# Shifting weight preparation between GpSimd, TensorE, ScalarE and VectorE in an attention plus two-MLP kernel, with a new written-out order

## The chip, the core and the metric

One Trainium2 core runs the whole program. Its engines are TensorE (PE in the profile, with its weight loads as PEld), VectorE (DVE), ScalarE (ACT), GpSimd (POOL) and SyncE (SP, which issues the DMAs). The metric is device time in microseconds (us). Three timed runs of the kernel before gave 652.4, 654.35 and 654.43 us, median 654.35. The profiled execution took 653.11 us, of which 651.3 us lie between its first and its last instruction.

## The reference

```
attention: q, k, v  (2 batches, 8 heads, 576 tokens, 64 wide)
  scores = q @ k^T / 8;  kth = 32nd largest of each row
  scores below kth -> -1e9;  attn = softmax;  x = attn @ v     -> 1152 tokens x 512
layer 1:  h = x @ w_in (512 x 2048);   g = max(0.01 h, h);          x = g @ w_out (2048 x 512)
layer 2:  h = x @ w_in2;               g = h * tanh(softplus(h));   out = g @ w_out2
```

## The kernel before

The 1152 tokens are nine tiles of 128, each with eight heads, so there are 72 slots (tile, head). For a slot PE makes 576 scores (line 676), ACT copies them to SBUF in two halves (678), and DVE finds the 32 largest: four `MAX8` (691), each of which yields eight, with three `MATCH_REPLACE8` (694) between them that strike out what was found. GpSimd makes two small scalars from the largest and the 32nd (709, 711), ACT masks and exponentiates (714, 715), PE multiplies with v. After a tile's eighth head DVE normalises its x (778), and the two layers follow, each in four groups: `ph` products (822 to 824) and `y` products (831 to 833). Every float32 operand there is split into a float16 high half and a float16 low half, and three products are summed.

The weights arrive as 16 groups q of 512 x 512 words (0 to 3 and 4 to 7 for layer 1, 8 to 11 and 12 to 15 for layer 2). Each word is 64 bits wide in memory, and the value is put together from its high and its low 32 bits. `load_w` does that in pieces of 1024 words per partition, as the tuple `CV` says for each group: with 1, DVE makes two passes over the high word (389, 395), ACT brings the top bits of the low word into place (382), and GpSimd adds them in, 256 elements at a time (`add`, 331). With 2, DVE makes its second pass as a bare mask (392), and GpSimd adds that too. With 0, DVE does it all in three passes (389, 395, 400), and neither ACT nor GpSimd takes part.

`split_w` takes a group's sum of squares on PE (`gram`, 411), reduces it over the partitions by a product with `ones` (415), makes a power-of-two scale from it and splits the group, as the tuple `LO` says. With 3, ACT writes the high half (433), GpSimd makes a diagonal matrix of the scale (431), PE forms the negated low half as diagonal times raw plus identity times high (436 in float32, 437), and ACT evicts it (438). With 0, ACT scales the raw words in place (459) and copies the high half out (460), and GpSimd subtracts the two (462, or 454 for four groups that are done in place).

The order on each engine is not left to a scheduler: `ORDER` lists for every engine the numbers of its instructions in the sequence in which they are to stand, and `put_in_order` ties each to the one ahead of it. So an engine whose next instruction waits does nothing else, even if later ones could run. Score buffers (`sc`) number three, so the scores of a slot can be copied out only when the slot three earlier has been masked.

Of the kernel before, what the change touches and what calls it, by code (L numbers as in the profile page):

```python
# [9 lines left out]
BF16 = mybir.dt.bfloat16  # L10
# [9 lines left out]
        """22 25 20+2 23 19 26+4 24 35+2 42+2 30 38 37 31 44 32 45+11 33 57+2 56 40 39 34 60 62 59 61 69 63+2 68 67 73  # L20
# [4 lines left out]
        186 185 187 183 189+2 188 191+3 195+2 194 197+4""",  # L25
    "Activation":
        """1 6 2 7 4 3 5 9 8 20 16 10+2 45+2 17 12 18+2 21 13+2 27+2 22 15 29 47 23 39 30 24+2 40 33 41 48+2 31 35 34
# [29 lines left out]
        865 868+4 874+2 879+2 876+3 881+5 889 886+3 890+6""",  # L57
    "Pool":
# [133 lines left out]
def topk_attention_moe_moe2_kernel(  # L192
# [17 lines left out]
    nc = tc.nc  # L210
    P = 128
# [43 lines left out]
    one = cpool.tile([P, 1], F32, name="one")  # L255
# [827 lines left out]
    n = NS  # L1083
# [36 lines left out]
```

## Time and profile before

| what | us |
|---|---|
| timed runs, median of 3 | 654.35 |
| profiled execution, whole | 653.11 |
| profiled execution, first to last instruction | 651.3 |
| busy: PE, DVE, ACT, POOL | 594.3, 541.7, 540.2, 400.7 |

An engine's busy time is the sum of the stretches in which it worked. PE's instructions overlap (each matmul of 128 columns is shown for 220 ns, while the next starts 56 ns later), so its share is read together with the distance between starts. The rows that follow are cut by stretch because different engines are full at different times. The clock (PEclk) is the granted TensorE clock: 1.00 is 2.4 GHz, 0.5 is 1.2 GHz.

### The profile page before, as it was taken

The page shows a single profiled execution, that of the slowest core. Times are in us where ns is not written, and L with a number is a line of the kernel's source. Part 1 is how long each engine was busy: PE and PEld are TensorE (multiplying, and loading weights), DVE is VectorE, ACT ScalarE, POOL GpSimd, SP SyncE. Part 2 cuts the span into 40 slices and gives each one's busy share as a digit, 9 for nine tenths or more (in the row PEclk, how much of TensorE's full clock was granted, in tenths as well). Part 3 has the DMA queues.
Part 4 walks back from the last instruction along what each step waited for, and adds up shares of the span by engine and source line. Part 5 has one row for each costly group of instructions (what it writes and reads, how often), then busy time and mean ns, then how long its engine had stood idle before and what let it go on. Part 6 is the DMA issues. An engine that isn't in the chain of part 4 may idle for free.

```text
span 651.3 us, 16588 instructions
## 1 busy us (share of the span) xinstructions
PE 594.3 (91%) x6420; PEld 434.6 (67%) x6420; DVE 541.7 (83%) x1172; ACT 540.2 (83%) x1011; POOL 400.7 (62%) x594
## 2 busy tenths in 40 slices
PE   2468778989798999999999999999999999999997
PEld 1234545567677887777687777767776877777673
DVE  3998999999999999999999999999999989320232
ACT  4679898999989999999987998897997898752663
POOL 2989986797967745755654566575656575631430
PEclk9999798989899999999999999999999999999999
DMA  8483466553354201444446224253455424210000
GB/s 272 149 314 129 148 209 207 169 166 130 130 165 147 97 23 33 80 82 109 90 77 117 48 60 81 54 84 74 91 71 92 85 48 77 56 33 18 17 2 33
DMA packets 109359, 66.22 MB, mean 102 GB/s; under 512 B 93792, under 2 KB 99936, under 8 KB 109280
## 3 DMA queue, kind: packets, MB, share of 16 engines
q1 hardware_dynamic: 109280, 65.16, 39.0%
q8 instruction: 50, 0.82, 0.5%
q14 instruction: 29, 0.24, 0.1%
HBM read 41.16 MB, written 2.36 MB: 67 GB/s over the span
## 4 chain that ended last, share of the span: by engine, by line
PE 51%; DVE 21%; ACT 18%; issue 4%; DMA 3%; POOL 1%; SPq 1%; POOLq 0%; DVEq 0%; ACTq 0%
DVE top L691 7%; PE ph L822 7%; PE ph L824 7%; PE ph L823 7%; DVE wk L694 7%; PE y L831 6%; PE y L833 6%; PE y L832 6%; PE sps L676 3%; ACT wk L715 2%; DVE warena L395 2%; PE lp L436 2%; DMA rawkr<-in_k_dram 1%; ACT sc L678 1%; DVE warena L389 1%
## 5 line engine op out<-in xcount | busy, mean ns | idle before, releaser
L822 PE MATMUL ph<-xt,warena 128*128 128x128 f16 x1152 | 202.9, 220 | 1.9 <-ACT lk L845 1.1
L823 PE MATMUL ph<-xt,warena 128*128 128x128 f16 x1152 | 203.9, 220 | 0.0
L824 PE MATMUL ph<-xt,warena 128*128 128x128 f16 x1152 | 203.1, 221 | 0.0
L691 DVE MAX8 top<-wk 128x8 f32<-128x576 f32 x216 | 160.7, 753 | 2.7
L331 POOL TENSOR_TENSOR warena<-warena 128x256 int32<-128x256 int32 x136 | 109.5, 832 | 19.3 <-ACT warena L382 6.6
L823 PEld LDWEIGHTS <-warena 128*128 128x128 f16 x1152 | 113.3, 98 | 8.9 <-issue 3.1
L822 PEld LDWEIGHTS <-warena 128*128 128x128 f16 x1152 | 113.5, 99 | 7.6 <-issue 1.4
L824 PEld LDWEIGHTS <-warena 128*128 128x128 f16 x1152 | 113.2, 99 | 2.0 <-issue 0.4
L831 PE MATMUL y<-warena,gg 128*128 128x512 f16 x288 | 109.3, 380 | 0.9 <-DVE gg L863 0.9
L832 PE MATMUL y<-warena,gg 128*128 128x512 f16 x288 | 109.2, 379 | 0.0
L833 PE MATMUL y<-warena,gg 128*128 128x512 f16 x288 | 109.2, 379 | 0.0
L694 DVE MATCH_REPLACE8 wk<-top,wk 128x576 f32<-128x576 f32 x144 | 106.7, 742 | 0.0
L676 PE MATMUL sps<-kst,qst 128*128 128x288 f16 (+1 forms) x320 | 64.3, 299 | 11.7 <-ACT sc L678 10.3
L714 ACT ACTIVATE wk<-sc,nb,iv 128x576 f32<-128x576 f32 x72 | 62.5, 868 | 13.4 <-POOL nb L709 13.3
L678 ACT COPY sc<-sps 128x288 f32<-128x288 f32 x144 | 55.3, 398 | 12.0 <-PE sps L676 11.3
L860 DVE SCALAR_TENSOR_TENSOR mc<-mc,gg 128x512 f32<-128x512 f32 x36 | 26.5, 736 | 45.0 <-ACT mc L859 44.8
L846 POOL TENSOR_TENSOR gg<-lk,gg 128x512 f16<-128x512 f32 x36 | 41.7, 1159 | 34.1 <-ACT lk L845 34.0
L715 ACT ACTIVATE wk<-wk,nb 128x576 f32<-128x576 f32 x72 | 56.1, 779 | 4.3 <-POOL nb L711 2.9
L691 DVE MAX8 top<-sc 128x8 f32<-128x576 f32 x72 | 53.9, 749 | 3.4 <-ACT sc L678 2.1
L694 DVE MATCH_REPLACE8 wk<-top,sc 128x576 f32<-128x576 f32 x72 | 53.4, 742 | 0.0
L709 POOL TENSOR_SCALAR nb<-top,iv 128x2 f32<-128x2 f32 x72 | 25.6, 356 | 39.0 <-DVE top L691 31.3
L831 PEld LDWEIGHTS <-gg 128*128 128x128 f16 x288 | 28.3, 98 | 31.0 <-issue 2.1
(186 smaller groups left out, 1430.3 us busy)
## 6 DMA issues: line engine op xcount, KB each, us to landing
warena<-in_moe_w_in_dram SPq DMA_DIRECT2D x16, 1024.0 KB, 5.4
warena<-in_moe_w_out_dram SPq DMA_DIRECT2D x13, 1024.0 KB, 4.9
warena<-in_moe_w_out_dram SPq DMA_DIRECT2D x6, 512.0 KB, 3.7
out_dram<-o SPq DMA_DIRECT2D x9, 256.0 KB, 2.3
rawkv<-in_v_dram SPq DMA_DIRECT2D x8, 256.0 KB, 3.4
qr<-in_q_dram SPq DMA_DIRECT2D x8, 256.0 KB, 3.6
warena<-held SPq DMA_DIRECT2D x8, 256.0 KB, 2.9
rawkr<-in_k_dram SPq DMA_DIRECT2D x6, 256.0 KB, 3.6
```

The lines of the kernel that those rows point to most:

```text
L331: nc.gpsimd.tensor_tensor(out=o[:, a:a + PIECE], in0=o[:, a:a + PIECE], in1=x[:, a:a + PIECE], op=ALU.add)
L676: nc.tensor.matmul(sps[p0:p0 + n, :HS], lhsT=lq[:, c, p0:p0 + n], rhs=rk[:, half * HS:(half + 1) * HS], start=(c == 0), stop=(c == 1))
L691: nc.vector.max(out=top[:, 8 * r:8 * r + 8], in_=src)
L694: nc.vector.match_replace(out=wk, in_to_replace=top[:, 8 * r:8 * r + 8], in_values=src, imm_value=NEG)
L714: nc.scalar.activation(e, sc, AF.Prelu, bias=nb[:, 1:2], scale=iv, alpha=1e30)
L715: nc.scalar.activation(e, e, AF.Exp, bias=nb[:, 2:3], accum_out=self.sums[:, h:h + 1])
L822: nc.tensor.matmul(o, lhsT=wb, rhs=xa, start=(c == 0), stop=False)
L823: nc.tensor.matmul(o, lhsT=wa, rhs=xb, start=False, stop=False)
L824: nc.tensor.matmul(o, lhsT=wa, rhs=xa, start=False, stop=(c == KC - 1))
L831: nc.tensor.matmul(y, lhsT=gb, rhs=whi(j), start=(g == 0 and f == 0), stop=False)
L832: nc.tensor.matmul(y, lhsT=ga, rhs=wlo(j), start=False, stop=False)
L833: nc.tensor.matmul(y, lhsT=ga, rhs=whi(j), start=False, stop=(g == FG - 1 and f == 3))
```

## The change

Three things change in the code, and the written-out order with them. The new file is 13 lines shorter above these places, so its line numbers are 13 lower: what was 389, 392, 395, 400, 462, 691 and 694 is 376, 379, 382, 387, 449, 678 and 681 in the new order's rows.

- `CV`: groups 1, 5, 6, 8, 10 and 12 go from 1 to 0, and group 3 from 2 to 0.
- `LO`: groups 1, 3, 5, 6 and 8 go from 3 to 0.
- The products with `ones`, which sum a per-partition number over the partitions for k, v, x and each weight group, take the upper 16 bits of both operands as bfloat16, in place of float32.

```diff
-    ones = one.to_broadcast([P, P])
+    ones = one.bitcast(BF16)[:, 1:2].to_broadcast([P, P])
...
     def total(part, n, where=ps_p, tag="p"):
...
-        nc.tensor.matmul(t[:, :n], lhsT=ones, rhs=part, start=True, stop=True)
+        nc.tensor.matmul(t[:, :n], lhsT=ones, rhs=part.bitcast(BF16)[:, 1::2], start=True, stop=True)
...
-    CV = (2, 1, 1, 2, 2, 1, 1, 1, 1, 1, 1, 1, 1, 1, 0, 1)
+    CV = (2, 0, 1, 0, 2, 0, 0, 1, 0, 1, 0, 1, 0, 1, 0, 1)
...
-    LO = (3, 3, 3, 3, 3, 3, 3, 3, 3, 3, 0, 0, 0, 0, 0, 0)
+    LO = (3, 0, 3, 0, 3, 0, 0, 3, 0, 3, 0, 0, 0, 0, 0, 0)
...
-        nc.tensor.matmul(gram[:, P:P + 1], lhsT=ones, rhs=part, start=True, stop=True)
+        nc.tensor.matmul(gram[:, P:P + 1], lhsT=ones, rhs=part.bitcast(BF16)[:, 1::2], start=True, stop=True)
...
 ORDER = {
     "SP":
-        """22 25 20+2 23 19 26+4 24 35+2 42+2 30 38 37 31 44 32 45+11 33 57+2 56 40 39 34 60 62 59 61 69 63+2 68 67 73
+        """21 20 22 19 25 28+2 27 26 23+2 35+2 42 38 43 37 31 44 30 45+2 48 47 34 49 51 50 52 55 54 53 32 39 56 33 58
...
```

Counted over the whole order, GpSimd loses 64 adds of 256 and five diagonals and gains 20 subtractions of 512; ACT loses 14 moves of low words (382), 20 evictions (438) and ten high halves (433) and gains ten scalings (459) and ten copies (460); PE loses 20 float32 diagonal products (436) and 20 identity products (437); DVE gains 14 third passes (400) and two second passes (395) and loses two masks (392).

On DVE, at the start of the program, from the second half of the first keys to the first `MAX8` on scores; before:

```order
L615 SCALAR_TENSOR_TENSOR qn<-qr,qs,qn 128x4x64
L389 TENSOR_SCALAR warena<-warena 128x1024
L392 TENSOR_SCALAR warena<-warena 128x1024
L389 TENSOR_SCALAR warena<-warena 128x1024
L395 SCALAR_TENSOR_TENSOR warena<-warena 128x1024
L389 TENSOR_SCALAR warena<-warena 128x1024
L264 TENSOR_SCALAR u<-tot 128x1
L267 TENSOR_SCALAR ks<-u 128x1
L395 SCALAR_TENSOR_TENSOR warena<-warena 128x1024
L271 TENSOR_SCALAR k_i<-u 128x1
L540 SCALAR_TENSOR_TENSOR kn<-rawkv,ks,kn 128x5x64
L691 MAX top<-sc 128x8 x2
```

and now:

```order
L602 SCALAR_TENSOR_TENSOR qn<-qr,qs,qn 128x4x64
L258 TENSOR_SCALAR k_i<-u 128x1
L376 TENSOR_SCALAR warena<-warena 128x1024
L379 TENSOR_SCALAR warena<-warena 128x1024
L602 SCALAR_TENSOR_TENSOR qn<-qr,qs,qn 128x4x64
L678 MAX top<-sc 128x8
L376 TENSOR_SCALAR warena<-warena 128x1024
L681 MATCH_REPLACE wk<-top,sc 128x576
L379 TENSOR_SCALAR warena<-warena 128x1024
L678 MAX top<-wk 128x8
L681 MATCH_REPLACE wk<-top,wk 128x576
L678 MAX top<-sc 128x8
```

Five passes over weights (389, 395 and the mask 392) stood between the second query half and the first search for maxima; now the search begins directly behind that half and the passes stand between its steps.

On DVE, further on among the weight groups, where searches and passes alternate; before:

```order
L694 MATCH_REPLACE wk<-top,wk 128x576
L389 TENSOR_SCALAR warena<-warena 128x1024
L264 TENSOR_SCALAR u<-gram 128x1
L395 SCALAR_TENSOR_TENSOR warena<-warena 128x1024
L691 MAX top<-wk 128x8
L264 TENSOR_SCALAR u<-qpart 128x1
L267 TENSOR_SCALAR qs<-u 128x1
L267 TENSOR_SCALAR w_s<-u 128x1
L694 MATCH_REPLACE wk<-top,wk 128x576
```

and now:

```order
L382 SCALAR_TENSOR_TENSOR warena<-warena 128x1024
L678 MAX top<-wk 128x8 x2
L681 MATCH_REPLACE wk<-top,wk 128x576 x2
L678 MAX top<-wk 128x8
L387 SCALAR_TENSOR_TENSOR warena<-warena 128x1024
L251 TENSOR_SCALAR u<-qpart 128x1
L376 TENSOR_SCALAR warena<-warena 128x1024
L681 MATCH_REPLACE wk<-top,sc 128x576
L254 TENSOR_SCALAR qs<-u 128x1
L678 MAX top<-wk 128x8 x2
L602 SCALAR_TENSOR_TENSOR qn<-qr,qs,qn 128x4x64
L382 SCALAR_TENSOR_TENSOR warena<-warena 128x1024
```

A piece of weights now takes three passes (376, 382 and 387) in place of two, and two searches stand interleaved more often than one behind itself.

On POOL, at the scalars of the first slots (709 and 711, now 696 and 698), with the adds (331, now 318) around them; before:

```order
L331 TENSOR_TENSOR warena<-warena 128x256 x2
L662 TENSOR_SCALAR iv<-k_i,qi 128x1
L331 TENSOR_TENSOR warena<-warena 128x256 x8
L431 TENSOR_SCALAR diag<-identf,w_s 128x128
L331 TENSOR_TENSOR warena<-warena 128x256 x2
L711 TENSOR_SCALAR nb<-nb 128x1
L331 TENSOR_TENSOR warena<-warena 128x256 x2
L709 TENSOR_SCALAR nb<-top,iv 128x2
L331 TENSOR_TENSOR warena<-warena 128x256
L711 TENSOR_SCALAR nb<-nb 128x1
```

and now:

```order
L696 TENSOR_SCALAR nb<-top,iv 128x2 x2
L698 TENSOR_SCALAR nb<-nb 128x1 x2
L449 TENSOR_TENSOR warena<-warena 128x512
L418 TENSOR_SCALAR diag<-identf,w_s 128x128
L449 TENSOR_TENSOR warena<-warena 128x512
L649 TENSOR_SCALAR iv<-k_i,qi 128x1
L449 TENSOR_TENSOR warena<-warena 128x512 x2
L318 TENSOR_TENSOR warena<-warena 128x256 x12
L696 TENSOR_SCALAR nb<-top,iv 128x2
L698 TENSOR_SCALAR nb<-nb 128x1
```

The two scalars of a slot now stand one behind the other, where adds and a diagonal stood between them, and subtractions of 512 (449) stand among the adds.

On PE the counts of layer products ahead of each slot's scores hardly move: ahead of slot 23's scores stood 312 `ph` and 50 `y` products, now 312 and 55; ahead of the last slot's 2652 and 624, now 2629 and 624, of 3456 and 864 in all. On SP the first keys are now the first two transfers; they were the third and fourth.

## Rows read from the trace of the kernel before

**Rows 1.** The page: busy time by engine, and the chain by engine

```profile
PE 594.3 (91%) x6420; PEld 434.6 (67%) x6420; DVE 541.7 (83%) x1172; ACT 540.2 (83%) x1011; POOL 400.7 (62%) x594
...
PE 51%; DVE 21%; ACT 18%; issue 4%; DMA 3%; POOL 1%; SPq 1%; POOLq 0%; DVEq 0%; ACTq 0%
```

**Rows 2.** Busy time by stretch: length; PE, PEld, DVE, ACT, POOL; clock; DMA

```profile
0.00:25.00 25.00, 7.44 (x43) 4.98 (x44) 13.47 (x26) 14.91 (x25) 10.56 (x17) 1.00 0.75 257
25.00:75.00 50.00, 35.58 (x198) 21.67 (x198) 46.40 (x91) 38.48 (x68) 46.14 (x65) 0.97 0.52 179
75.00:150.00 75.00, 64.59 (x413) 42.48 (x412) 71.56 (x151) 68.87 (x117) 60.61 (x87) 0.93 0.56 185
150.00:225.00 75.00, 67.64 (x659) 53.46 (x658) 73.89 (x158) 71.51 (x132) 58.95 (x73) 0.98 0.41 137
225.00:556.00 331.00, 328.40 (x4098) 247.83 (x4097) 315.35 (x709) 294.42 (x585) 193.56 (x316) 1.00 0.39 73
556.00:651.30 95.30, 90.62 (x1017) 64.14 (x1014) 21.08 (x42) 52.06 (x89) 30.88 (x39) 1.00 0.11 26
```

**Rows 3.** The chain of work from 150 to 160: start, length, what

```profile
154.23 0.77 ACT wk L715 x2
155.00 1.04 ACT warena L459
```

**Rows 4.** Lines, shapes apart: count, busy us, mean ns, idle before

```profile
L331 POOL TENSOR_TENSOR warena<-warena 128x256 int32<-128x256 int32 x136 | 109.5, 832 | 19.3 <-ACT warena L382 6.6 <-DVE warena L392 4.6 <-DVE w_s L267 2.6
...
L436 PE MATMUL lp<-warena,diag 128*128 128x512 f32 x80 | 44.5, 656 | 3.3 <-POOL diag L431 2.0 <-ACT warena L438 1.3
...
L382 ACT ACTIVATE warena<-warena 128x1024 int32<-128x1024 uint16 x28 | 32.0, 1159 | 0.0
L395 DVE SCALAR_TENSOR_TENSOR warena<-warena 128x1024 int32<-128x1024 int32 x23 | 31.0, 1348 | 0.3
...
L389 DVE TENSOR_SCALAR warena<-warena 128x1024 int32<-128x1024 int32 x29 | 27.0, 932 | 3.9 <-PE lp L436 1.7 <-DMA warena<-in_moe_w_in_dram 1.6 <-PE lp L437 0.3
...
L438 ACT ACTIVATE warena<-lp 128x512 f16<-128x512 f32 x40 | 23.4, 596 | 1.6 <-PE lp L437 1.6
L433 ACT ACTIVATE warena<-warena,w_s 128x1024 f16<-128x1024 f32 x20 | 23.0, 1152 | 0.6 <-DVE w_s L267 0.5
...
L392 DVE TENSOR_SCALAR warena<-warena 128x1024 int32<-128x1024 int32 x6 | 6.5, 1086 | 0.1
...
L462 POOL TENSOR_TENSOR warena<-warena 128x512 f16<-128x512 f32 x4 | 5.6, 1416 | 0.0
...
L459 ACT ACTIVATE warena<-warena,w_s 128x1024 f32<-128x1024 f32 x2 | 2.3, 1153 | 0.0
...
L460 ACT CAST warena<-warena 128x1024 f16<-128x1024 f32 x2 | 2.1, 1075 | 0.0
```

**Rows 5.** DVE in order of time, 81 to 92: start, length, what

```profile
81.45 0.74 DVE L694 MATCH_REPLACE8 wk<-top,sc 128x576 f32<-128x576 f32 x1
82.23 0.76 DVE L691 MAX8 top<-wk 128x8 f32<-128x576 f32 x1
...
85.17 1.65 DVE L395 SCALAR_TENSOR_TENSOR warena<-warena 128x1024 int32<-128x1024 int32 x1
86.73 0.75 DVE L691 MAX8 top<-wk 128x8 f32<-128x576 f32 x1
87.41 0.13 DVE L264 TENSOR_SCALAR u<-qpart 128x1 int32<-128x1 int32 x1
...
91.20 1.23 DVE L395 SCALAR_TENSOR_TENSOR warena<-warena 128x1024 int32<-128x1024 int32 x1
```

**Rows 6.** PE in order of time around one sum over partitions

```profile
417.47 0.29 PE L676 MATMUL sps<-kst,qst 128*128 128x288 f16 x1
417.60 0.28 PE L285 MATMUL tot<-xpart,one 128*128 128x1 f32 x2
417.74 0.22 PE L822 MATMUL ph<-xt,warena 128*128 128x128 f16 x1
```

More of the change, by code (lines that the diff above doesn't have):

```diff
@@ L19 @@
     "SP":
-        """22 25 20+2 23 19 26+4 24 35+2 42+2 30 38 37 31 44 32 45+11 33 57+2 56 40 39 34 60 62 59 61 69 63+2 68 67 73
[4 rows of a table removed]
-        186 185 187 183 189+2 188 191+3 195+2 194 197+4""",
-    "Activation":
-        """1 6 2 7 4 3 5 9 8 20 16 10+2 45+2 17 12 18+2 21 13+2 27+2 22 15 29 47 23 39 30 24+2 40 33 41 48+2 31 35 34
[29 rows of a table removed]
-        865 868+4 874+2 879+2 876+3 881+5 889 886+3 890+6""",
-    "Pool":
-        """0 2+3 8 5+2 12 15 31 28 32+2 29 10 9 7 14 11 13 19 17 30 16 18 20 23 35 24 34 21+2 37 26 39 25 36 38 60 40
[19 rows of a table removed]
-        574+2 578 576+2 579+3 584 582+2 585 587 586 588+3""",
-    "DVE":
-        """1+4 7 9 0 5 8 6 10 21+2 11 23+2 47+3 12+2 50 14+2 17 31 18 33 19 16 20 41 30 35+2 32 34 43 40 45 25 42 26 51
[32 rows of a table removed]
-        900 891 901 903 899 902 916 935 917+2 921+2 924 923 919 913 925 920 926+9 936+4""",
-    "PE":
-        """0+27 40+2 38+2 27 42+4 28+5 57+4 33+5 46 96+2 71+17 47+5 98+2 88 90 61+4 91 89 52+5 135+16 92 151 94 93
[55 rows of a table removed]
-        5825+36 5921+12 5982+11 5934+34 5994+12 5968+14 6006+12 5993 6018+36 6102+12 6054+48 6114+96""",
+        """21 20 22 19 25 28+2 27 26 23+2 35+2 42 38 43 37 31 44 30 45+2 48 47 34 49 51 50 52 55 54 53 32 39 56 33 58
[4 rows of a table added]
+        176 180+2 174 182 179 184 186 185 187 183 189+2 188 191+3 195+2 194 197+4""",
+    "Activation":
+        """1+2 6 4 3 7 5 8+2 16+2 20 18 10+2 19 21 12 14 13 27 45 22 15 28+2 39 30 40 23 31 25 36 32 24 41+2 46 33 47
[28 rows of a table added]
+        835+7 843+4 850+2 847 852+2 855 854 856+3 860 859 861 865 862+3 866+6""",
+    "Pool":
+        """0 2+3 7 5 8 12+2 16 6 11 10 9 14 17 15 18 23 19 24 20 29+2 28 31 26+2 25 34 36+2 35 33 21 32 22 38 65+2 39
[17 rows of a table added]
+        525+2 529 527+2 530+4 535 534 538 536+2 539+3""",
+    "DVE":
+        """1 0 2+2 5 7 6 9 8 10 4 21+2 11 17 23 18 24 19+2 31 30 33 12 32 14 13 47 35 34 36 15 40 50 42 16 44 48 37 49
[33 rows of a table added]
+        931 935+3 939 938 932+3 940+3 949 943 953 944+5 950+3""",
+    "PE":
+        """0+19 38+4 19+8 42+4 27+6 71+12 57+2 33+5 83+5 46 59+2 96+4 61+4 135+8 66 47+5 65 88 52+4 100+2 56 143+7
[44 rows of a table added]
+        5942+12 5894+48 5954+23 6002+3 6014+12 5977+25 6005+9 6062+12 6026+36 6074+96""",
 }
```

265 rows, old and new, of the table ORDER are left out of this document.

## Prediction

> **What bounds the kernel now.** I read the page's busy shares first, then the table of busy time by stretch, then the chain of work, then the prices of the lines that the change touches. The shares alone mislead: PE has 91%, DVE and ACT 83% each [rows 1]. By stretch the picture is another [rows 2]. In the first 25 us little runs, and DVE is idle for 25 - 13.5 = 11.5. From 25 to 225 DVE works 46.4 + 71.6 + 73.9 = 191.9 of 200, more than any other engine, ACT 178.9, PE 167.8, GpSimd 165.7. From 225 to 556 PE is busy for 328.4 of 331 and DVE for 315.4. After 556 DVE has little left, and PE runs the rest of the two layers, 90.6 of 95.3. So the first third is set by DVE: it must search the scores and unpack the weights at once. The middle is set by PE and DVE together, tied by the written-out order and by the three score buffers. The end is PE's backlog, whose length is fixed by how many layer products the order puts ahead of the last slot's scores.
>
> That last point decides how an early delay travels. The new order has nearly as many layer products ahead of slot 23's scores as the old (312 and 55 against 312 and 50) and ahead of the last slot's (2629 and 624 against 2652 and 624). PE therefore has as much left behind slot 23 as before, and it had next to no idle time there. A slot 23 that comes later by some microseconds moves the end by about as many, and one that comes earlier the other way. I work out slot 23, at about 225 us, and add what changes behind it.
>
> **What DVE is given.** Sixteen more two-input passes over 1024 words and two masks fewer, all ahead of slot 23. At the mean durations that is 16 x 1.348 - 2 x 1.086 = 19.4 us [rows 4]. An instruction that does not need the one ahead of it starts 0.07 before that one's end (86.73 + 0.75 against 87.41) [rows 5], so DVE's time grows by less: 19.4 - 16 x 0.07 = 18.3. With the quicker pass of 1.23 it would be 17.5 less that overlap, 16.4. I take 18.3, bounds 16.4 and 19.4.
>
> **What DVE gets back in the first third.** Four items.
> - An instruction right behind its own input starts 0.04 after that one's end (81.45 + 0.74 against 82.23), others 0.07 before [rows 5]; each such pair costs 0.11. Up to slot 23's search the old order has 51 instructions that wait for the one directly ahead on DVE, the new one 15: 36 x 0.11 = -4.0. Behind that, 178 and 163: -1.7.
> - The same pass took 1.65 at 85.17 and 1.23 at 91.20 [rows 5]; GpSimd was at work for 165.7 of those 200 us [rows 2]. GpSimd loses 64 x 0.832 and gains 20 x 1.416, net 24.9 us less, 15% of its load [rows 4]. I take -2, bounds 0 and -4.
> - At the start the first keys are now the first transfer, and the first search stands behind fewer passes. The 11.5 us of idle time [rows 2] shrink by the one or two transfers that no longer go first and by gaps that the search fills: -1.5, bounds 0 and -3.
> - Of the 8.1 us in which DVE is idle from 25 to 225, 1.7 + 0.3 are waits of the first pass for the diagonal products (436, 437) that still read the raw buffers [rows 4]; half of those products go. The rest are small waits for ACT and GpSimd, which both get lighter. I take -2.5, bounds 0 and -6.
>
> Sum for slot 23: 18.3 - 4.0 - 2 - 1.5 - 2.5 = +8.3.
>
> The Trainium skill ("GPSIMD Engine Reference", section Key points) says that GpSimd shares its SBUF interfaces with VectorE and contends with VectorE instructions that have two SBUF inputs, as all the added passes have. The trace agrees that such passes vary, 1.23 to 1.65 [rows 5]. If every added pass met it at 1.65, the first term would be 16 x 1.65 - 2.2 = 24.2 instead of 19.4, and the forecast about 5 us higher; I keep the mean of 23 measured ones, which has the contention of a busier GpSimd in it.
>
> **What the other engines lose.** ACT: 14 x 1.159 + 20 x 0.596 + 10 x 1.152 go, 10 x 1.153 + 10 x 1.075 come, net -17.4 us [rows 4]. PE: 40 pieces of float32 diagonal at 0.656 shown, 26 us [rows 4]. GpSimd -24.9. Nearly all of it lies ahead of 225, where DVE is the fullest, so I count it at nothing beyond the 2.5 above. If the cover fails, that is, if ACT and not DVE sets that stretch, it is the rival below.
>
> **The sums in bfloat16.** One float32 sum holds PE from 417.47 + 0.12 to 417.74, two pieces of 0.13 and 0.14 with their weight loads [rows 6]; one piece of it instead saves about 0.11, bounds 0 and 0.2. There are 34 sums besides the 16 of the weight groups, most of them behind 225, where PE has no slack: 25 x 0.11 = -2.8. As PE and DVE are both nearly full there, the two late savings (-1.7 on DVE, -2.8 on PE) do not add up; I take -3 together, bounds 0 and -6. What the different sequence does to the small waits of the middle I put at 0, bounds -5 and +5.
>
> **Sum.** +8.3 - 3 = +5.3 on the profiled execution's 653.1, so 658.4; that execution lay 1.2 below the median of the three runs, well inside their spread of 2. I say 658.5. Its own range, from the terms' bounds taken two or three at a time, is 653 to 666.
>
> **Rivals.**
> 1. Relief wins, and the kernel gets faster. Between 150 and 225 the chain runs over ACT [rows 3], which is busy for 71.5 of 75 [rows 2]; it loses 17.4 us, and GpSimd's two scalars of a slot stand closer together in the new order. DVE was idle for 11.5 + 8.1 = 19.6 us up to 225. Its work there grows by 18.3 - 4.0 - 2 = 12.3. So if its idle time falls below 7.3, slot 23 comes earlier than before; then lighter engines also feed the 15.7 us of idle time that DVE has from 225 to 556. Half of these back, and the 3 of above, give 653 - 3 - 8 = 642 at best; I put this case at 646. For it: the chain. Against it: DVE itself is busy for 73.9 of 75 in the same stretch, and the first 7 or 8 us of the program can't be filled.
> 2. Nothing to be seen. The idle time up to 225 falls by about 9 in place of 4: 12.3 - 9 - 3 is 0, so 653, within 651 to 655. For it: three engines get lighter at once. Against: most of that idle time is the start.
> 3. The full price, and more. The waits stay, contention stays, and PE, with less to do early, is granted the lower clock more often; in 75 to 150 the mean grant was already 0.93 [rows 2], and full speed came back as PE filled up. 19.4 - 1.7 = +17.7, and if PE's 64.6 busy us of that stretch [rows 2] grew by a tenth and came through, 6 more: 671 to 677. For it: PE falls from 168 to about 142 busy us. Against: PE does not set that stretch.
>
> **How the numbers follow.** Forecast 0.50, rival 1 0.28, rival 2 0.17, rival 3 0.05. A measurement of this kernel tells about 0.3% (2 us) from no change. Forecast: mostly slower by more, 0.05 of it within 2 us. Rival 1: faster, 0.02 of it within. Rival 2: 0.13 within, the rest to either side by 0.02. So faster 0.28, same 0.20, slower 0.52. The range for 8 in 10 reaches down to rival 1's 646 and up past the forecast's own end to 668.
>
> **What would show it.** Right: DVE busy for about 560 us in all, idle for under 5 from 25 to 225, slot 23's search some 8 us later, and from there PE busy without gaps to an end later by 5. GpSimd and ACT lighter by 25 and 17 ahead of 225 with more idle time there. The sums over partitions: half as many pieces, each gap on PE shorter by 0.1. Wrong: slot 23's search at or before its old time (rivals 1 and 2); or DVE waiting for ACT or GpSimd more than before (rival 3); or an end that moves by less than slot 23 does, which would mean that the middle had slack that I did not see.

## The result and the profile after

The changed kernel takes 644.89 us (median of 6 runs, 643.25 to 650.57) against 654.39 for the kernel before in the same group of runs. The ratio is 0.9883, 95% interval 0.9859 to 0.9907 (the plain quotient of the two medians is 0.9855). In another group the changed kernel took 644.6 (0.987 [0.9848, 0.9893]). The forecast, 658.5 and slower, is wrong in sign, and the time lies just below its range of 646 to 668.

The profiled execution took 646.44 us, its span 644.5. The page's busy times and chain after, answering to [rows 1]:

```profile
PE 584.9 (91%) x6310; PEld 429.5 (67%) x6310; DVE 540.1 (84%) x1186; ACT 528.1 (82%) x987; POOL 384.6 (60%) x545
...
PE 53%; DVE 24%; ACT 9%; issue 4%; POOL 4%; DMA 4%; SPq 2%; POOLq 0%; DVEq 0%; ACTq 0%
```

The same stretches as in [rows 2], with the same columns:

```profile
0.00:25.00 25.00, 6.08 (x36) 3.60 (x36) 14.40 (x36) 13.16 (x22) 11.57 (x21) 1.00 0.77 257
25.00:75.00 50.00, 38.42 (x202) 23.77 (x202) 47.86 (x94) 38.43 (x67) 32.06 (x43) 0.90 0.53 175
75.00:150.00 75.00, 59.42 (x356) 42.31 (x357) 69.73 (x143) 59.74 (x101) 53.64 (x58) 0.68 0.51 176
150.00:225.00 75.00, 67.51 (x637) 52.78 (x635) 74.18 (x162) 69.51 (x123) 55.73 (x68) 0.91 0.44 148
225.00:556.00 331.00, 329.99 (x4149) 248.07 (x4148) 315.39 (x717) 299.82 (x597) 205.47 (x326) 1.00 0.41 75
556.00:644.50 88.50, 83.51 (x936) 58.95 (x934) 18.57 (x38) 47.46 (x80) 26.15 (x32) 1.00 0.09 22
```

DVE has more long passes and is busy for 1.6 us less in all. Up to 225 us it works 206.2 in place of 205.3; up to the start of slot 23's search, which is what the forecast's 12.3 more was about, it works 210.4 (to 229.3) in place of 205.3 (to 225.0), 5.1 more. PE's clock has fallen from 0.93 to 0.68 between 75 and 150, and from 225 on PE is full: 1.0 us idle of 331 in place of 2.6 [rows 2].

DVE's passes over 1024 words, and GpSimd's adds, in the groups by line and shape, answering to [rows 4]:

```profile
L318 POOL TENSOR_TENSOR warena<-warena 128x256 int32<-128x256 int32 x72 | 57.5, 824 | 33.5 <-DVE ks L254 7.3 <-DVE w_s L254 5.4 <-ACT warena L420 5.3
L382 DVE SCALAR_TENSOR_TENSOR warena<-warena 128x1024 int32<-128x1024 int32 x25 | 30.6, 1227 | 0.0
...
L376 DVE TENSOR_SCALAR warena<-warena 128x1024 int32<-128x1024 int32 x29 | 21.6, 750 | 2.9 <-DMA warena<-in_moe_w_in_dram 2.6 <-PE lp L423 0.2
...
L387 DVE SCALAR_TENSOR_TENSOR warena<-warena 128x1024 int32<-128x1024 int32 x15 | 18.6, 1246 | 0.0
...
L379 DVE TENSOR_SCALAR warena<-warena 128x1024 int32<-128x1024 int32 x4 | 3.6, 902 | 0.1
```

They sum (the adds left out) to 74.4. Those of before in [rows 4] sum to 64.5, and the kernel before had one long third pass, which stands there in no row:

```profile
L400 DVE SCALAR_TENSOR_TENSOR warena<-warena 128x1024 int32<-128x1024 int32 x1 | 1.2, 1212 | 0.0
```

So the change in passes costs 74.4 - 65.7 = 8.7 us, not 19.4, because a first pass takes 0.750 in place of 0.932 and a second one 1.227 in place of 1.348.

The traces show where a first pass gets its length. Of the kernel before, a long one with what GpSimd did meanwhile, and a short one beside which GpSimd ran nothing:

```profile
83.84 1.29 DVE L389 TENSOR_SCALAR warena<-warena 128x1024 int32<-128x1024 int32 x1
83.14 2.58 POOL L331 TENSOR_TENSOR warena<-warena 128x256 int32<-128x256 int32 x3
114.02 0.68 DVE L389 TENSOR_SCALAR warena<-warena 128x1024 int32<-128x1024 int32 x1
```

In the kernel before, 21 of the 29 first passes lie over at least a twentieth of their length beside GpSimd's adds or subtractions on weights and take 1.03 on average, the other 8 take 0.68; in the changed kernel 11 do (0.86), and 18 do not (0.69). In all the runs of this document together, no first pass or mask without such an add or subtraction beside it is longer than 0.72, and the longest with one is over 1.6. So the passes became shorter as fewer of them met that work; that this alone did it, no run shows.

The forecast was made for slot 23's search. Its first `MAX8` and that of slot 71, the last, in the kernel before and in the changed one:

```profile
225.00 0.74 DVE L691 MAX8 top<-sc 128x8 f32<-128x576 f32 x1
549.25 0.74 DVE L691 MAX8 top<-sc 128x8 f32<-128x576 f32 x1
```

```profile
229.30 0.74 DVE L678 MAX8 top<-sc 128x8 f32<-128x576 f32 x1
544.12 0.74 DVE L678 MAX8 top<-sc 128x8 f32<-128x576 f32 x1
```

Slot 23's search is 4.3 later, not 8.3; from it to the last search it takes 314.8 in place of 324.2, 9.4 less; and what follows takes 1.6 less. The first third did become later. All of the gain lies behind it.

To compare the experiments, which exchange the sequence at slot 24, all runs are read at two other places: PE's first score product of slot 24 and of slot 71. After, these two rows of PE's timeline show them (line 663 is what was 676):

```profile
226.31 0.41 PE L663 MATMUL sps<-kst,qst 128*128 128x288 f16 x2
```

```profile
538.17 0.65 PE L663 MATMUL sps<-kst,qst 128*128 128x288 f16 x4
```

In the kernel before they begin at 227.2 and 546.0. Slot 24's scores have thus not become later, although slot 23's search has: the new sequence puts them 3.0 ahead of that search, the old one had them 2.2 behind it. The stretch between takes 311.9 in place of 318.8, and the rest of the program is 1 us longer, as 23 `ph` products, about 0.056 each, have moved there from ahead of slot 71.

All times that follow are device times (median; ratio to the kernel before in the same group of runs, with its 95% interval) and, from the profiled execution, slot 24's scores, the stretch from slot 24 to 71 ("middle"), and the rest.

| run | start | sequence behind slot 24 | sums | us | ratio | slot 24 | middle | rest |
|---|---|---|---|---|---|---|---|---|
| before | old | old | f32 | 654.39 | 1 | 227.2 | 318.8 | 105.3 |
| e2 | old | old | bf16 | 652.71 | 1.0001 [0.9985, 1.0017] | 223.0 | 320.3 | 105.4 |
| e4 | old | new | f32 | 650.5 | 0.996 [0.9946, 0.9975] | 225.9 | 314.1 | 106.4 |
| e7 | old | new | bf16 | 644.39 | 0.9865 [0.984, 0.9889] | 227.2 | 310.0 | 106.0 |
| e8 | new | old | f32 | 659.54 | 1.0109 [1.0079, 1.0138] | 233.0 | 322.8 | 105.3 |
| e3 | new | old | bf16 | 655.44 | 1.0031 [1.0013, 1.0049] | 228.1 | 320.9 | 104.7 |
| e1 | new | new | f32 | 653.69 | 1.0009 [0.9997, 1.0022] | 228.1 | 315.4 | 106.8 |
| changed | new | new | bf16 | 644.89 | 0.9883 [0.9859, 0.9907] | 226.3 | 311.9 | 106.4 |
| changed, again (a0) | new | new | bf16 | 644.6 | 0.987 [0.9848, 0.9893] | 223.8 | 312.5 | 106.4 |

Runs are named by the first part of their labels. The kernel before took 652.4 to 653.2 in the other groups, so across groups the ratios are compared. "New start" is the changed `CV` and `LO` with the new order up to slot 24. One profiled execution of the same start can differ from another by some microseconds (223.0 and 227.2 in e2 and e7), so small differences are taken from the ratios. The profiled execution of e8 was the slowest of its six (663.72), that of e4 the fastest (648.28).

### The profile page after: what moved, and what is told of

Read it like the earlier page. It is cut to its first block, busy times and chain, and to the rows that moved or that the text cites. A ratio compares the mean times of both kernels' runs of the same rounds, so it can differ in the third digit from the quotient of the medians.

```text
span 644.5 us, 16247 instructions
## 1 busy us (share of the span) xinstructions
PE 584.9 (91%) x6310; PEld 429.5 (67%) x6310; DVE 540.1 (84%) x1186; ACT 528.1 (82%) x987; POOL 384.6 (60%) x545
## 4 chain that ended last, share of the span: by engine, by line
PE 53%; DVE 24%; ACT 9%; issue 4%; POOL 4%; DMA 4%; SPq 2%; POOLq 0%; DVEq 0%; ACTq 0%
DVE top L678 8%; DVE wk L681 7%; PE ph L809 7%; PE ph L810 7%; PE ph L811 7%; PE y L818 6%; PE y L820 6%; PE y L819 6%; PE sps L663 3%; PE av L720 2%; DVE warena L382 2%; PE lp L423 2%; PE gram L398 1%; DVE warena L376 1%; ACT wk L701 1%
## 5 line engine op out<-in xcount | busy, mean ns | idle before, releaser
L810 PE MATMUL ph<-xt,warena 128*128 128x128 f16 x1152 | 199.8, 220 | 0.0
L809 PE MATMUL ph<-xt,warena 128*128 128x128 f16 x1152 | 199.7, 220 | 0.0
L811 PE MATMUL ph<-xt,warena 128*128 128x128 f16 x1152 | 199.2, 220 | 0.0
L681 DVE MATCH_REPLACE8 wk<-top,wk 128x576 f32<-128x576 f32 x144 | 106.8, 742 | 0.0
L318 POOL TENSOR_TENSOR warena<-warena 128x256 int32<-128x256 int32 x72 | 57.5, 824 | 33.5 <-DVE ks L254 7.3
L701 ACT ACTIVATE wk<-sc,nb,iv 128x576 f32<-128x576 f32 x72 | 62.5, 869 | 12.4 <-POOL nb L696 12.3
L833 POOL TENSOR_TENSOR gg<-lk,gg 128x512 f16<-128x512 f32 x36 | 43.8, 1220 | 26.2 <-ACT lk L832 25.3
L696 POOL TENSOR_SCALAR nb<-top,iv 128x2 f32<-128x2 f32 x72 | 30.6, 424 | 36.4 <-DVE top L678 29.7
```

The costliest lines, as they stand in the source:

```text
L318: nc.gpsimd.tensor_tensor(out=o[:, a:a + PIECE], in0=o[:, a:a + PIECE], in1=x[:, a:a + PIECE], op=ALU.add)
L681: nc.vector.match_replace(out=wk, in_to_replace=top[:, 8 * r:8 * r + 8], in_values=src, imm_value=NEG)
L701: nc.scalar.activation(e, sc, AF.Prelu, bias=nb[:, 1:2], scale=iv, alpha=1e30)
L809: nc.tensor.matmul(o, lhsT=wb, rhs=xa, start=(c == 0), stop=False)
L810: nc.tensor.matmul(o, lhsT=wa, rhs=xb, start=False, stop=False)
L811: nc.tensor.matmul(o, lhsT=wa, rhs=xa, start=False, stop=(c == KC - 1))
```

## The experiments

### The three parts alone and together

The sums and the sequence were exchanged in either kernel.

```diff
e1: changed kernel      - lhsT=ones (bf16), rhs=part.bitcast(BF16)[:, 1::2]   + lhsT=ones (f32), rhs=part
e2: kernel before       - lhsT=ones (f32), rhs=part   + lhsT=ones (bf16), rhs=part.bitcast(BF16)[:, 1::2]
e3: changed kernel      ORDER: as it is up to slot 24, then the sequence of the kernel before
e4: kernel before       ORDER: as it is up to slot 24, then the sequence of the changed kernel
```

> The changed kernel with the sums over partitions back in float32, all else as changed. Theory M (the new sequence behind slot 23 loses fewer waits) expects only the sums' own price on PE, 25 to 34 sums at 0.11 us, so 2 to 4 us above the changed kernel's 644.9: 647 to 649. Rival S (the bfloat16 sums shorten PE's stream and the chains of scale factors, and that is what the middle regains) expects most of the 9.5 us back: 651 to 654. Rival E (the lighter first third clears a backlog, and the middle only profits) expects as M.

> The kernel before with its own order, only the sums over partitions in bfloat16. Theory M: 2 to 4 us below 654.4, so 650 to 652. Rival S: 645 to 648. Rival E: 650 to 652.

> The changed code; its own new order on every engine up to 226 us (slot 24's scores on PE), from there each engine's remaining instructions in the sequence of the kernel before. Theory M: slot 23's search stays at about 229, the middle from there to slot 71's search takes about 322 again instead of 315 (the sums still save 3), end 651 to 654. Rivals S and E: the middle stays at 315, end 645 to 647.

> The code before; its own old order up to 227 us, from there each engine's remaining instructions in the new sequence. Theory M: slot 23's search at 225 as before, the middle takes about 317, and the end comes at 645 to 648, 6 to 9 us below the kernel before. Rival S: no gain, 652 to 655, since the sums are in float32. Rival E: 652 to 655, since the first third is the old one.

Same code, only the later sequence undone (e3 against the changed kernel): the middle is 320.9 in place of 311.9. So the sequence wins there. But e4 gets only 2.6 us from it by the ratio, and the sums, worth 0.0 in the old program (e2), are worth 8 in the new one (e1). The parts do not add up. Theory M had the middle of e3 but missed e1 (647 to 649 expected) and e4 (645 to 648); rival S had e1 and missed e2; rival E missed e3. The other two combinations, the changed kernel again, and a test of GpSimd's load, whose adds stood, by the trace, between 27.8 and 148.9 us and not up to 225:

```diff
a0: changed kernel, nothing changed
e7: e4 with the sums of e2
e8: e3 with the sums of e1
e9: changed kernel
+    spare = cpool.tile([P, 112], I32, name="spare")
+    nc.gpsimd.memset(spare, 1)
+    for i in range(60):        # placed by ORDER between GpSimd's own instructions
+        nc.gpsimd.tensor_tensor(out=spare, in0=spare, in1=spare, op=ALU.add)
```

> The changed kernel itself once more, as the measure for the others of this group: 643 to 647, ratio to the kernel before 0.986 to 0.991.

> The kernel before with its own weight preparation and its own order up to slot 24, the new sequence behind that, and the bfloat16 sums: everything of the change but CV, LO and the first third's order. Theory I (interaction): the new later sequence keeps PE full from 225 on, so only there do shorter sums on PE count; moving weight work by CV and LO with the new start costs 2 to 3 us (e3 against e2: 2.7; e1 against e4: 3.2). Then slot 24's scores stand at about 223 as in the run with the old order and bfloat16 sums, the stretch from slot 24 to 71 takes 312, the rest 106: span 641, time 641 to 644, faster than the changed kernel by 2 to 4. Rival: the lighter GpSimd and ScalarE of the changed CV and LO are what lets the new sequence gain; then the sums add next to nothing to the run with old start and new sequence (650.5): 648 to 650.

> The changed CV and LO with the new order up to slot 24, the old sequence behind it, and float32 sums: CV, LO and the start alone. Theory I: behind slot 24 the old sequence leaves PE waits into which longer sums fall, so the time is that of the same kernel with bfloat16 sums (655.4) within 2 us: 654 to 657, slower than before. Rival: the sums are worth 8 us wherever the new start stands: 661 to 664.

> The changed kernel with sixty idle adds of 112 int32 words on GpSimd between its own instructions from about 45 to 225 us (on a spare tile that nothing else reads), which by the 0.83 of an add of 256 should be some 25 us: as much GpSimd work as the change took away there. Theory P (GpSimd's load sets how long VectorE's passes last): the passes go back from 1.23 to about 1.35 and from 0.75 to about 0.93, 47 second and third passes and 31 first ones together 6 to 9 us more; slot 24's scores 3 to 8 us later and the end as many: 648 to 653. Rival: the passes were shorter for another reason (they stand elsewhere, ScalarE is lighter): mean durations within 0.03 of the changed kernel's and 644 to 647.

**e7 and e8.** With its own weight preparation and its own first third, the kernel before reaches 644.39 as soon as it has the new sequence and the bfloat16 sums (Theory I had expected 2 to 4 below the changed kernel; it is level). So `CV`, `LO` and the new start contribute nothing to the final gain. By the ratios they cost 7 us alone (e8), 2 with bfloat16 sums (e3 against e2), 3 with the new sequence (e1 against e4) and nothing that can be told with both (a0 against e7). Theory I had 654 to 657 for e8 and missed by 2.5. Of the eight combinations only the two with both the new sequence and bfloat16 sums gain more than 3 us.

Why the two need each other is seen in the stretch from 225 to 556. Kernel before with shorter sums (e2), then the same start with the new sequence, float32 (e4) and bfloat16 (e7):

```profile
225.00:556.00 331.00, 324.25 (x4077) 242.66 (x4075) 310.78 (x699) 292.98 (x583) 194.90 (x316) 1.00 0.40 74
```

```profile
225.00:556.00 331.00, 329.07 (x4146) 249.23 (x4144) 311.33 (x706) 295.86 (x590) 200.22 (x318) 1.00 0.38 74
```

```profile
225.00:556.00 331.00, 329.75 (x4145) 247.28 (x4144) 311.37 (x709) 298.52 (x594) 202.58 (x321) 1.00 0.41 75
```

In the old sequence PE is idle for 2.6 [rows 2] with float32 sums and for 6.8 with the shorter ones: what PE saves it waits away, and the middle stays (318.8, 320.3). In the new sequence PE is full with either, 1.9 and 1.3 idle, so the middle shrinks by what PE saves, 314.1 to 310.0. With the new start the old sequence leaves PE idle for 7.4 and 8.0 (e8, e3), the new one for 1.1 and 1.0 (e1, changed):

```profile
225.00:556.00 331.00, 323.58 (x4024) 243.82 (x4022) 313.19 (x707) 293.73 (x585) 194.78 (x315) 1.00 0.38 72
```

```profile
225.00:556.00 331.00, 322.99 (x4019) 240.78 (x4018) 315.23 (x709) 294.74 (x586) 193.94 (x315) 1.00 0.39 73
```

PE's longest waits in e2 from 227 to 556 (us in total, times, longest) are these; `lk` and `mc` are what ACT reads out of the `ph` products' buffers in layers 1 and 2, and the transfer of `pts` brings the transposed softmax weights:

```profile
PE av L760 <- DMA pts<-warena: 2.4, 4, 1.2
PE ph L822 <- ACT lk L845: 1.7, 2, 1.1
PE ph L822 <- ACT mc L855: 1.2, 2, 0.6
```

None of the three is left in e7, where PE's longest is 0.6. Idle time is not all of the difference, though. In the new sequence 23 `ph` products (1.3 us) stand behind the middle, and from the kernel before to e4, or e2 to e7, 5 `y` products (1.1) stand ahead of it: these work elsewhere and are no gain. Idle time and moved products together make 3.1 of 4.7 (before to e4), 7.9 of 10.2 (e2 to e7), 7.6 of 7.4 (e8 to e1) and 8.3 of 9.0 (e3 to changed); what is over in the first two is not traced. In all runs the old sequence's middle is 318.8 to 322.8 whatever the sums; the new one's is 314.1 to 316.2 with the 34 sums in float32 and 310.0 to 314.7 with them in bfloat16 (means 315.2 and 312.4). The two ranges touch, so this rests on the means. 23 of the 34 sums stand there, so one is worth 2.8 / 23 = 0.12.

**e9.** The 60 adds took 30.9 us, and the time rose by 15 to 659.48 (1.0086 [1.0058, 1.0113]), far above what either theory had. Passes, the dummies, and what DVE waited for from 25 to 226 us in that run (us in total, times, longest):

```profile
L375 DVE SCALAR_TENSOR_TENSOR warena<-warena 128x1024 int32<-128x1024 int32 x25 | 32.6, 1306 | 0.0
L1070 POOL TENSOR_TENSOR spare<-spare 128x112 int32<-128x112 int32 x60 | 30.9, 515 | 2.4
L369 DVE TENSOR_SCALAR warena<-warena 128x1024 int32<-128x1024 int32 x29 | 22.0, 763 | 4.7 <-DMA warena<-in_moe_w_in_dram 2.2 <-POOL warena L442 2.1 <-PE lp L416 0.3
...
L380 DVE SCALAR_TENSOR_TENSOR warena<-warena 128x1024 int32<-128x1024 int32 x15 | 18.8, 1261 | 0.0
```

```profile
DVE gram L393 <- PE gram L391: 4.2, 6, 1.0
DVE qn L595 <- ACT qn L594: 3.1, 2, 2.6
DVE warena L369 <- POOL warena L442: 2.1, 2, 1.4
```

and PE's longest row of waits for GpSimd there:

```profile
PE lp L416 <- POOL diag L411: 7.5, 4, 3.9
```

These passes together grew by 2.6 us. The second pass went up as theory P said (1.227 to 1.306, half of it by a single pass of 2.2); the first one did not (0.750 to 0.763). The idle adds are no stand-in for the real ones there: four first passes with four fifths or more of their length beside an idle add, and no real one beside them, took 0.68 to 0.72. The rest of the loss is waiting: PE for GpSimd's diagonal (7.5 us, 1.3 without the adds), DVE for PE, ACT and GpSimd. Slot 24 came at 236.9, 10.6 later than in the changed kernel's profile, the middle took 311.8 as without the adds, and the span grew by 10.2: a delay of the first third reaches the end unchanged, as the prediction assumed. (The profiled execution, 656.66, was 2.8 below the median of e9, hence 10 here and 15 there; against the profile of a0, slot 24 is 13.1 later and the span 12.1 longer.) So GpSimd's load, whose relief the prediction counted at "nothing beyond the 2.5", is not free in the new start. What the same load cost in the old start no run shows.

### Where the sums count, and the clock

The middle gives the sums 2.8 us of their 8. The other part lies ahead of slot 24, with the new start only. I split the sums, and gave PE more to do, since the clock had fallen.

```diff
e10: changed kernel, the 16 sums of the weight groups (line 402) in f32, the 34 others in bf16
e11: changed kernel, the 34 others (line 272) in f32, those 16 in bf16
e12 (e13: 12 for 5): changed kernel, behind each of the first three chunks of 15 groups' gram
+            for i in range(5 if c < 3 and q < 15 else 0):
+                nc.tensor.matmul(gram[:, :P], lhsT=identh, rhs=none, start=False, stop=False)   # none is zeros
```

> The changed kernel with the 16 sums of the weight groups back in float32, the 34 others in bfloat16. Theory K: in the new first third the granted clock is low (0.68 to 0.77 from 75 to 150), each float32 sum is longer there, and VectorE waits for it behind every weight group; so slot 24's scores stand 2 to 4 us later than the 223.8 to 226.3 of the changed kernel, the stretch from slot 24 to 71 keeps its 312: 646 to 649. Rival: sums count only where PE is full, behind slot 24: 644 to 646.

> The changed kernel with the 34 sums of k, v, q and x back in float32, the 16 of the weight groups in bfloat16. Theory I: most of the 34 stand behind slot 24, where the new sequence keeps PE full; the stretch from slot 24 to 71 becomes 315 as with all sums in float32, and the end 3 to 6 us later: 648 to 651. Rival: the weight groups' sums are what counts: 644 to 646.

> The changed kernel with 225 idle products of 128 columns (a matrix of zeros, added to each of 15 weight groups' sums of squares in three lots of five) on TensorE ahead of 225 us, some 13 to 25 us of its work there. Theory K (the low granted clock of the new first third costs time): the clock of 25 to 225 rises from 0.82 to 0.88 to above 0.9 and slot 24's scores come 2 to 4 us earlier: 640 to 643. Rival: the clock costs nothing, since VectorE sets that stretch; the idle products only lengthen PE's queue: 645 to 650.

> The same with 540 idle products, in lots of twelve, some 30 to 60 us of PE's work. Theory K: the clock goes on rising, to 0.95 or more, but the products now fill PE's idle time of 25 to 225 (32 us), so the gain is used up: 642 to 648. Rival: PE becomes the engine that sets the first third: 655 to 670.

Measured: e10 649.65 (0.9961 [0.9943, 0.9978]), slot 24 at 231.0, middle 312.3. e11 653.53 (1.0016 [0.9998, 1.0034]), 230.5 and 314.5. e12 654.58 (1.0033 [1.0017, 1.0049]), 233.9; e13 669.61 (1.0255 [1.0233, 1.0276]), 249.1. Both e10 and e11 are slower than their theories had. The middle behaves as theory I says. But either half of the sums alone makes slot 24 late by at least as much as both (228.1 in e1): not a price per sum, then, but something that is either lost or kept whole. e12 and e13 missed both of their theories' better times, and they did not test the clock: the fillers stood in front of the gram that DVE needs (its wait for it went from 3.3 to 9.2 us in e12), and the mean clock from 25 to 225 hardly moved (0.82 and 0.88 in the changed kernel's two profiles, 0.86 in e12). They show that PE's work there is no more free than GpSimd's.

The chain of work shows it. Changed kernel from 206 us, then e11:

```profile
206.70 0.45 PE pt L712 x4
207.23 0.60 ACT pts L713
207.87 1.10 PE av L720 x8
...
209.40 0.06 PE ph L811
```

```profile
208.37 0.87 PE pt L712 x4
209.31 0.59 ACT pts L713
209.95 1.97 PE av L720 x8
...
214.16 0.11 PE ph L809
```

The same products take twice as long in e11 until 214.2. In all runs of the table above with the new start the granted clock falls between 187 and 192, among PE's waits; in the three bfloat16 ones it is back by 205, in e10 and e11 only at 214 to 215, and in e1 and e8 it falls again (208.7 to 212.1, 211.2 to 214.6). Why it lasts longer with float32 sums is not shown. From slot 18's to slot 24's scores takes 44.7 (changed), 44.6 (a0), but 48.6 (e10), 49.2 (e11), 47.8 (e1). To tell the clock from the sums, PE's waits were filled with products that nothing reads:

```diff
e14: changed kernel; 72 products, put by ORDER ahead of the waits at 185, 188, 190 and 197 us (16, 11, 28, 17)
e15: e1 with the same 72
e16: e1 with 120: also ahead of the waits at 195 (15), 204 (22) and 209 (11)
+                    fill = ps_y.tile([P, 512], F32, tag="y", name="fill")
+                    for i in range(72):
+                        nc.tensor.matmul(fill[:, :P], lhsT=identh, rhs=identh, start=True, stop=True)
```

> The changed kernel with 72 idle products (identity times identity into a free PSUM tile that nothing reads) put on TensorE directly ahead of four instructions that wait there between 185 and 198 us: 16, 11, 28 and 17, each lot by 0.06 a product as long as the wait that it fills (1.05, 0.73, 1.74 and 1.1). Theory K (the clock that falls to 0.5 at 190 and is back at 206 costs time there): PE no longer idle, the clock stays at 1.00 from 185 to 206, slot 24's scores come 2 to 4 us earlier, 641 to 643.5. Rival: the first third is set by VectorE, and PE at half speed only shortens its own waits: 644 to 646.5, with the clock at 1.00 or not.

> The changed kernel with all sums back in float32 (653.7 without more) and the same 72 idle products. Theory K: float32 sums cost most of their 8 us in the first third because the full clock comes back at 215 in place of 206; with the waits filled the clock does not fall there, slot 24's scores come 3 to 6 us earlier than the 228.1 of that kernel, and only the middle's 3 us and less remain: 647 to 650. Rival: the sums' cost is on PE's stream itself: 652 to 655.

> The changed kernel with all sums in float32 as in the run before (653.5), and three lots of idle products more, 120 in all: also ahead of a wait of 1.06 at 195.4, of 1.5 at 204.0 and of 0.73 at 208.6. In all runs with the new first third the stretch from the scores of slot 18 to those of slot 24 takes 44.6 to 44.8 where the clock is full from 206 on, and 47.1 to 49.2 where it is at 0.5 for most of 206 to 214, whatever it was from 185 to 205. Theory K2 (a low clock costs time only from 206 to 214, where PE is waited for): if the clock is now full from 206 to 214, that stretch falls from 48.1 to 45 and the time to 649 to 651; if the fall only moves on to 214 or later, likewise. Rival (float32 sums are late there by themselves): 48 and 653 or more, with the clock full.

The stretches 185 to 206 and 206 to 214 (columns as in [rows 2]; the clock is the number behind the five engines) in the changed kernel, e14, e11, e15 and e16:

```profile
185.00:206.00 21.00, 15.69 (x100) 12.79 (x99) 20.37 (x48) 19.69 (x38) 15.71 (x19) 0.67 0.58 189
206.00:214.00 8.00, 7.27 (x102) 6.71 (x102) 7.97 (x18) 7.80 (x13) 5.13 (x6) 1.00 0.62 199
```

```profile
185.00:206.00 21.00, 16.97 (x160) 13.57 (x159) 21.00 (x49) 19.20 (x37) 16.36 (x19) 0.92 0.53 193
206.00:214.00 8.00, 7.37 (x104) 6.96 (x105) 7.97 (x18) 7.97 (x15) 4.55 (x6) 1.00 0.59 179
```

```profile
185.00:206.00 21.00, 15.82 (x92) 13.04 (x92) 19.66 (x48) 19.19 (x37) 15.28 (x19) 0.63 0.57 193
206.00:214.00 8.00, 7.27 (x44) 6.50 (x44) 7.37 (x17) 5.64 (x9) 3.11 (x5) 0.50 0.58 183
```

```profile
185.00:206.00 21.00, 15.96 (x173) 13.38 (x172) 21.00 (x44) 19.82 (x37) 16.14 (x19) 1.00 0.50 176
206.00:214.00 8.00, 7.27 (x52) 6.70 (x52) 8.00 (x22) 6.20 (x9) 4.19 (x6) 0.59 0.74 232
```

```profile
185.00:206.00 21.00, 18.11 (x207) 15.57 (x207) 21.00 (x49) 19.37 (x37) 16.02 (x18) 1.00 0.52 183
206.00:214.00 8.00, 7.99 (x115) 7.59 (x115) 7.97 (x18) 7.97 (x15) 4.52 (x6) 1.00 0.57 174
```

| run | us | ratio | clock 185:206, 206:214 | slot 18 to 24 |
|---|---|---|---|---|
| changed | 644.89 | 0.9883 [0.9859, 0.9907] | 0.67, 1.00 | 44.7 |
| e14 | 646.76 | 0.9917 [0.9884, 0.995] | 0.92, 1.00 | 44.8 |
| e11 | 653.53 | 1.0016 [0.9998, 1.0034] | 0.63, 0.50 | 49.2 |
| e15 | 653.47 | 1.0015 [0.9995, 1.0034] | 1.00, 0.59 | 48.1 |
| e16 | 651.22 | 0.9988 [0.9971, 1.0005] | 1.00, 1.00 | 45.5 |

Theory K fell in its first form: a clock of 0.92 in place of 0.67 from 185 to 206 is worth nothing (e14), and in e15 the fillers only moved the fall to 207. In its second form it held for the stretch. With float32 sums and the clock kept full to 214 the stretch takes 45.5 in place of 48.1 (theory 45, rival 48); the time, 651.2, is just above the theory's 649 to 651 and about 2 below e15 by the ratios. From slot 18's to slot 23's scores, ahead of the place where the sequences part, the runs without more work on GpSimd or in front of the gram agree: 38.5 to 39.2 with a full clock from 206 to 214 (changed, a0, e3, e14, e16), 41.5 to 42.9 with a lower one there (e1, e8, e10, e11, e15). From 206 to 214 ACT is busy for 7.80 to 7.97 of 8 us at full clock and for 5.64 to 6.20 at 0.50 to 0.59: it waits for PE, and DVE for it, as these two rows show, from just behind that stretch (ACT in e15, DVE in e11; in brackets the wait before them):

```profile
215.23 0.40 ACT L655 COPY sc<-sps 128x288 f32<-128x288 f32 x1 [1.42 <-PE sps L653]
```

```profile
218.83 0.15 DVE L251 TENSOR_SCALAR u<-qpart 128x1 int32<-128x1 int32 x1 [2.06 <-ACT qn L277]
```

So most of what the float32 sums lose ahead of slot 24 is not their own duration: with the low clock gone from 206 to 214, 2.6 of the 3.4 us by which e15's stretch is longer than the changed kernel's came back. (In e9 the clock was low from 206 to 216 too and the stretch from slot 18 to 24 took 46.1, to slot 23 40.0, so the price depends on what else waits.) Of e16's distance to the changed kernel, 651.2 - 644.9 = 6, the middle (316.2 against 311.9) makes 4 in the profiles; the rest is not traced.

## Why the prediction was wrong, point by point

- **"What the different sequence does to the small waits of the middle I put at 0, bounds -5 and +5": the step that failed.** By the prediction's own marks the stretch from slot 23's search to the last one is 9.4 shorter, and this turned the sign. Read at PE's scores, the middle is 5.5 shorter with float32 sums (mean of 315.2 against 320.8) and 8.2 with bfloat16 ones; about 2 of that are products that now stand outside it. Over the eight combinations PE is idle from 225 to 556 for 2.6 to 8.0 in the old sequence and for 1.0 to 1.9 in the new one. The order's listing showed nearly the same counts of layer products ahead of slots, and I took that for the same waits.
- **The sums at 0.11 each, 2.8 in all: the size was right where PE is full** (0.12 each, 2.8). It was wrong to add them to the old sequence, where they give 0.0 (e2): there PE waits for the slots' chain and for ACT (the waits shown for e2).
- **Slot 23 later by 8.3: too large, but fair for the weights alone.** Its search is 4.3 later in the changed kernel (1.8 in a0, against the same 225.0). With float32 sums it starts at 231.1 and 232.5 with the new start (e1, e8) and at 225.0 and 222.6 with the old one (before, e4), 8.0 later on average. Two terms were mis-sized. The passes were priced at 19.4, with "I take -2" for contention, and cost 8.7, since fewer of them met GpSimd's work on weights: 0.18 less on 29 first passes, 0.12 on 25 second ones, and 0.1 on the third ones, which had been priced as second ones. And the bfloat16 sums, priced for the middle alone, counted here too: in the changed kernel the clock is full again by 205, and a full clock from 206 to 214 is worth some 3 us of that stretch (2.6 from e15 to e16).
- **"I count it at nothing beyond the 2.5 above": not borne out for the new start.** It was argued from DVE's busy share of the stretch. A DVE that is busy for 192 of 200 is not alone on the path: 31 us more on GpSimd cost 15 (e9), 25.5 us of idle products on PE cost 10 (e12).
- **A late slot 23 moves the end by as many: held** (e9: 10.6 at slot 24, 10.2 at the end).
- **Rivals.** Rival 1's time, 646, is nearly the measured one, but not by its mechanism, so that is luck: it was to decide where DVE's idle time up to slot 23 fell below 7.3, and that time is 18.9 (229.3 - 210.4), and slot 23's search came later, not earlier. Its second half, waits between 225 and 556 that come back, is what happened, but on PE and from the sequence (e7 has it without the lighter engines). Rival 3's lower clock came (0.68 in place of 0.93); no run tests what it costs between 75 and 150, and from 185 to 206 it cost nothing that e14 shows. The chances were wrong in giving a new order no case of its own.

## What to carry to other kernels

Price a change of a written-out order apart from the change of work that comes with it: here the order gave the gain, together with the shorter sums, and the moved weight work gave none of it; an instruction saved on an engine counted only under the sequence that kept that engine full. Follow a forecast at the place for which it was made: slot 24's scores stood still while slot 23's search came later. Read "busy for 96%" as a share and not as a bound: adding work on the lighter engines shows at once whether the path runs over them too. When small edits cost far more than their duration and do not add up, look for something that they switch, and compare the granted clock in windows of a few microseconds.

## What the runs showed of the chip that was not expected

- In the changed kernel the granted clock fell from 1.00 to 0.5 (1.2 GHz) at about 191, among PE's waits of 1.05, 0.73 and 1.74 us between 185 and 191.6. With products in those waits it did not fall there; it fell at 199 for 3.4 us in e14 and at 207 in e15, behind waits that were left, and in e16, where more were filled, not between 185 and 225.
- What a low clock costs went by its place: 0.67 in place of 0.92 from 185 to 206 nothing that the stretch shows (44.7 and 44.8), 0.59 in place of 1.00 from 206 to 214 2.6 us (e15, e16).
- DVE's second pass took 1.348 us before, 1.306 with the idle adds and 1.227 after: longer, the more of it lies beside GpSimd's adds on weights and its idle ones (on average 33%, 25% and 11% of the pass, worked out from the starts and ends in the three traces). The three means agree with the rule that the prediction cited from the Trainium skill ("GPSIMD Engine Reference", section Key points), for passes with two inputs; from one pass to the next the link is loose.
- A first pass has one input, and it was lengthened most: 0.67 to 0.69 alone and up to 1.5 beside GpSimd's adds or subtractions on weights in the kernel before. The idle adds of e9, on a small tile of their own, did not do that.
